# Spectral filter plus dense layers on one core: spectral groups of six PSUM banks, second-layer sums in halves of one bank, a new fixed order

## The chip, the cores and the metric

The kernel runs on one core of a Trainium2 chip. The metric is the device time of one execution in microseconds (us); the time given for a kernel is the median of its timed runs. The times in a profile are those of one further execution, recorded by the hardware profiler.

## The reference

One sequence of 2048 rows and 640 columns goes through a layer norm. The result `xn` feeds two branches, and the sum of both and of `x` is the output (bf16). Branch A is a filter in the frequency domain: a real 2-D Fourier transform over rows and columns, a product with complex weights (2048 x 321), and the inverse transform. Branch B is two dense layers with a gelu between them.

```python
def _A_ref(x, w_r, w_i):
    X = jnp.fft.rfft2(x.astype(jnp.float32), axes=(-2, -1))
    X = X * (w_r + 1j * w_i)
    return jnp.fft.irfft2(X, s=(S, D), axes=(-2, -1)).astype(jnp.bfloat16)
def _B_ref(x, w1, b1, w2, b2):
    h = _gelu(jnp.einsum("bsd,df->bsf", x, w1) + b1)      # 640 -> 1536
    return jnp.einsum("bsf,fd->bsd", h, w2) + b2          # 1536 -> 640
xn = _layernorm(x)
return x + _A_ref(xn, ...) + _B_ref(xn, ...)
```

## The kernel before

All matrix work is done by TensorE (PE) in bf16 with sums in PSUM, which has eight banks of 512 fp32 columns. The 2048 rows are 16 row tiles of 128.

**Head.** SyncE (SP) issues nearly all loads: x in pieces, the first layer's weights `W1` in five pieces of 128 input columns (`load_w1(0)` to `load_w1(4)`), tables, filter weights `Wf`, second-layer weights `W2`. VectorE (DVE) takes the statistics and normalises; row tiles 0 to 3 are transposed by PE (line 710), tiles 4 to 15 by DMA. PE starts with 38 idle matmuls on `warm`.

**First layer** (`ps<-xnT,W` in the profile). Per block of two or four row tiles and per 128 of the 1536 hidden columns, five matmuls of 256 or 512 columns into one bank (`hps`), then a gelu on ScalarE (ACT, line 770). In block 0 the sums advance piece by piece of `W1`.

**Filter.** A length-128 transform (`aps`, with `gtab`) for pairs of row tiles; then, in fixed chain, three kinds of groups, each written by PE to several banks and evacuated to SBUF by VectorE and ScalarE (lines 557 and 558):
- `bps`, the forward width transform (`five` with `etab`): chunks of the sequence (16 in all) against a table of 640 columns. The 640 inputs are four matmuls of 128 rows and 160 columns per chunk, and a remainder of 32 rows, whose matmuls run as 32-row tiles of the array, four at a time.
- `cps`, the forward small transform (`mtab`): matmuls of 32 x 32 and 322 columns on the 16 tiles of the array; VectorE then multiplies by the filter (lines 837, 841).
- `dps`, the inverse small transform (`ntab`), 320 columns; results are transposed by DMA (line 862).

After all of these, `eps` is the inverse width transform (`five` with `getab`), again 16 chunks; VectorE folds its output (lines 887, 892).

`bps` and `eps` work in six groups of two or three chunks (`GROUPS`), `cps` and `dps` in eight groups of 32 matmuls each; every group takes four banks, always among banks 0 to 3. `hps` and the second layer take banks 4 to 7 (`ZONE`).

**Second layer** (`ps<-W,gT`). Per row tile 12 contraction steps of 640 columns, which a bank does not hold, so each step is a matmul of 512 and one of 128 in two banks (`sums`). For nine row tiles (`KEEP`) the sum is formed early (`kps`) and added by VectorE to x + b2 (line 939). At the end a last transform with `htab` goes into the bank (`fps`), VectorE adds (line 948), and SP stores. Row tile 15 is done in pieces of 320, 160 and 160 columns.

**Order.** The program records every operation; `ORDER` gives, by number, the order on each of the five engines, and `Pool.find` gives each operation its banks. Semaphore waits follow from the data and bank dependencies. Each engine works strictly in its order, so that an operation that waits holds up all behind it. Operations of PE among themselves need no wait.

Of the kernel before, what the change touches and what calls it, by code (L numbers as in the profile page):

```python
# [123 lines left out]
class Pool:  # L124
# [34 lines left out]
    "sp": """8 13 14 17 15 16 19 18 21 22 20 27 30 23 26 28 153 155 166 168 32 31 35 46 48 37 179 181 192 194 38 39  # L159
41 34 44 33 29 52 49 40 205 219 221 207 43 42 50 45 51 47 36 54 508 506 505 507 529 531 530 532 554 553 53 555  # L160
556 578 577 580 579 597 642 606 623 633 669 659 678 741 695 750 732 715 766 705 775 782 789""",
    "pe": """7 117 55 119 278 260 122 233 251 242 124 269 234 270 243 252 261 281 254 236 235 279 253 263 272 245 264 273 237 282 275 138
# [8 lines left out]
713 776 777 764 770 778 771 779 772 773 780 783 784 785 786 787""",  # L171
    "act": """12 9 118 56 123 139 258 142 276 259 277 267 250 268 249 292 319 240 241 295 135 313 134 136 322 316 310 307 151 298 301 289
# [3 lines left out]
767 670 609 645 644 680 681 717 753""",  # L176
    "dve": """0 58 57 59 61 62 63 115 116 121 120 66 65 125 67 70 69 137 71 127 126 140 128 130 131 129 144 143 74 76 73 77
# [6 lines left out]
781 788""",  # L184
    "pool": """10 11 3 1 2 60 5 64 6 68 72 79 86 93 4 100 107 25 114 24 589 687 615 625 651 707 661 697 724 743 635 599
759 734 768 671""",
# [29 lines left out]
class Sched:  # L216
# [195 lines left out]
    def emit(self, es, last):  # L412
# [53 lines left out]
def bass_parallel_sum__spectral_gfnet__dense_activation_gelu__prompt_kernel(  # L466
# [21 lines left out]
    with ExitStack() as es:  # L488
# [33 lines left out]
        xb3 = sb("Xb", [128, 6 * 2 * KP])  # L522
# [3 lines left out]
        U2 = sb("U2", [128, 2 * D])  # L526
# [3 lines left out]
        YO, Y2, YF = 0, 6 * D, 9 * D  # L530
# [6 lines left out]
        p_xn, p_x1, p_xf, p_xb, p_y, p_t, p_z, p_u = Pool(2), Pool(1), Pool(2), Pool(2), Pool(2), Pool(2), Pool(2), Pool(3)  # L537
# [453 lines left out]
```

## Time and profile before

| | |
|---|---|
| median of three timed runs | 148.43 us (148.29 to 148.77) |
| span of the profiled execution, first to last instruction | 146.2 us |
| PE / VectorE / ScalarE / GpSimd busy | 140.4 / 110.9 / 81.1 / 23.7 us |
| granted TensorE clock | 1.000 |

The profiled execution's own time is given as its span alone; the timed median is 2.2 us longer. A line of the profile's groups has the line of the code, engine, operation, output<-inputs, shape (partitions x elements), count, then busy us, mean ns of one, and the idle time before it with what ended it. A timeline line has start, length, engine, line and the same names; `x32` joins 32 instructions of a kind. Matmuls are pipelined, so that one of 512 columns has a duration of 379 ns although the next starts much earlier; the ends of matmuls are modelled. All PE work of the kernel but the transposes stands under one line, that of the helper.

### The profile page before, as it was taken

To read this page: it belongs to the slowest core of one execution; us is meant where nothing else is said; L and a number is where in the kernel's file an instruction comes from. 1 tells how busy PE (TensorE), PEld (TensorE's weight loads), DVE (VectorE), ACT (ScalarE), POOL (GpSimd) and SP (SyncE) were. 2 spreads that over 40 slices of the span, in tenths; PEclk is the share of its full clock that TensorE was granted. 3 is DMA by queue.
4 is the path that set the end of the run, shared out by engine and by line. 5 is a ranking of instruction groups with operands and counts; after the bars stand their busy time and mean duration, and the time that the engine had idled before them with its cause. 6 is when DMAs were issued, how large, how long until landed. Compare 5 with 4: busy or idle time off the path is not lost.

```text
span 146.2 us, 4076 instructions
## 1 busy us (share of the span) xinstructions
PE 140.4 (96%) x1702; PEld 91.3 (62%) x1720; DVE 110.9 (76%) x233; ACT 81.1 (55%) x145; POOL 23.7 (16%) x40
## 2 busy tenths in 40 slices
PE   7999999999999999999999999999999999999993
PEld 7788998988455464457554645554446766556572
DVE  1799999999953459799877967982203998998982
ACT  3208999999989769763555633225476655201000
POOL 2330401304200009220200040000063700000000
DMA  4999998998999676968446844462569885103234
GB/s 105 328 394 354 319 164 197 203 175 229 241 238 160 162 195 137 242 126 167 89 92 128 56 95 89 46 142 56 91 129 225 178 188 180 45 4 137 90 135 135
DMA packets 30842, 23.63 MB, mean 162 GB/s; under 512 B 20457, under 2 KB 26857, under 8 KB 30697
## 3 DMA queue, kind: packets, MB, share of 16 engines
q1 hardware_dynamic: 28432, 17.81, 52.6%
q0 software_dynamic: 2368, 5.57, 17.6%
q8 instruction: 13, 0.21, 0.6%
q14 instruction: 5, 0.03, 0.1%
q10 hardware_dynamic: 24, 0.00, 0.0%
HBM read 13.54 MB, written 2.62 MB: 111 GB/s over the span
## 4 chain that ended last, share of the span: by engine, by line
PE 92%; DMA 4%; issue 1%; SPq 1%; DVE 0%
PE ps L546 91%; DMA W<-in_B_w_dram 4%; SPq L541 1%; PE ps L710 0%; DVE W L948 0%
## 5 line engine op out<-in xcount | busy, mean ns | idle before, releaser
L546 PE MATMUL ps<-xnT,W 128*128 128x256 bf16 (+2 forms) x384 | 58.8, 300 | 0.2
L546 PE MATMUL ps<-W,gT 128*128 128x512 bf16 (+3 forms) x380 | 55.7, 292 | 1.6 <-issue 1.1
L546 PEld LDWEIGHTS ps<-W,gT 128*128 128x128 bf16 x396 | 30.3, 98 | 23.4 <-issue 1.9
L546 PEld LDWEIGHTS ps<-xnT,W 128*128 128x128 bf16 x384 | 33.3, 98 | 16.4 <-issue 1.7
L770 ACT ACTIVATE gT<-ps,b1col 128x256 bf16<-128x256 f32 (+1 forms) x72 | 35.3, 558 | 6.8 <-PE ps L546 6.5
L666 DVE BATCH_NORM_STATS2 stats<-X 128x6 f32<-128x320 bf16 x32 | 13.9, 475 | 2.9 <-DMA X<-in_A_x_dram 2.9
L557 ACT ACTIVATE Wf<-ps 128x960 bf16<-128x960 f32 (+1 forms) x8 | 7.0, 902 | 13.7 <-PE ps L546 13.7
L933 POOL DMA_DIRECT2D X<-in_A_x_dram x8 | 7.1, 1132 | 40.5 <-DMA Wf<-in_A_w_r_dram 17.2
L837 DVE TENSOR_TENSOR T<-Y,Wf 128x1288 bf16<-128x1288 bf16 x16 | 12.7, 825 | 0.1
L670 POOL TENSOR_TENSOR rstd<-mv,mhalf 128x2 f32<-128x2 f32 (+1 forms) x10 | 7.2, 717 | 27.5 <-DVE mv L668 27.3
L557 ACT ACTIVATE Xb<-ps 128x960 bf16<-128x960 f32 (+1 forms) x7 | 7.7, 1106 | 6.7 <-PE ps L546 6.7
L933 POOL DMA_DIRECT2D xnT<-in_A_x_dram x8 | 7.5, 1154 | 24.2 <-ACT xnT L915 24.2
L558 DVE CAST Y<-ps 128x644 bf16<-128x644 f32 x8 | 6.5, 827 | 5.4 <-PE ps L546 5.4
L557 ACT ACTIVATE XV<-ps 128x1280 bf16<-128x1280 f32 (+3 forms) x10 | 9.5, 963 | 0.7 <-PE ps L546 0.7
L558 DVE CAST Wf<-ps 128x640 bf16<-128x640 f32 (+1 forms) x4 | 4.0, 990 | 7.6 <-PE ps L546 7.6
L558 DVE CAST Xb<-ps 128x960 bf16<-128x960 f32 (+1 forms) x5 | 5.9, 1178 | 4.1 <-PE ps L546 4.0
L726 DVE TENSOR_TENSOR T<-T 128x512 bf16<-128x512 bf16 (+1 forms) x32 | 8.5, 311 | 0.0
L691 DVE TENSOR_SCALAR T<-X,mv,rstd 128x640 bf16<-128x640 bf16 (+2 forms) x17 | 7.1, 430 | 0.9 <-POOL rstd L670 0.7
L546 PE MATMUL ps<-getab,XV 32*128 32x160 bf16 (+1 forms) x128 | 7.5, 241 | 0.0
L948 DVE TENSOR_TENSOR W<-ps,X 128x640 bf16<-128x640 f32 x8 | 6.5, 822 | 1.1 <-PE ps L546 1.1
L546 PEld LDWEIGHTS ps<-getab,XV 32*128 32x128 bf16 (+1 forms) x128 | 6.5, 146 | 1.3
L887 DVE TENSOR_TENSOR Wf<-Wf 128x960 bf16<-128x960 bf16 (+1 forms) x12 | 7.0, 597 | 0.4 <-ACT Wf L557 0.3
(52 smaller groups left out, 133.4 us busy)
## 6 DMA issues: line engine op xcount, KB each, us to landing
X<-in_A_x_dram POOLq DMA_DIRECT2D x8, 320.0 KB, 4.3
xnT<-in_A_x_dram POOLq DMA_DIRECT2D x8, 320.0 KB, 5.2
out_dram<-W SPq DMA_DIRECT2D x15, 160.0 KB, 1.8
X<-in_A_x_dram SPq DMA_DIRECT2D x7, 320.0 KB, 7.0
W<-in_B_w_dram SPq DMA_DIRECT2D x5, 384.0 KB, 5.9
W<-in_B_w_dram SPq DMA_DIRECT2D x4, 480.0 KB, 7.8
Wf<-in_A_w_i_dram SPq DMA_DIRECT2D x6, 160.5 KB, 5.4
Wf<-in_A_w_r_dram SPq DMA_DIRECT2D x6, 160.5 KB, 4.8
```

What stands on the lines that cost most here:

```text
L546: ins = e.matmul(o_, lhsT=lw, rhs=rh, start=st, stop=sp_, skip_group_check=True)
L557: return e.activation(dst(), src(), ACT.Copy, scale=scale)
L558: return e.tensor_copy(dst(), src())
L666: st_op[c] = K.op([("dve", 0.393)], pr, lambda e, _, c=c, h=h: e.bn_stats(stats[:, c, 6 * h:6 * h + 6], view(X, c * D + H2 * h, [[1, H2]]) ...
L670: K.op([("pool", 0.65)], 500, lambda e, _, a=a, b=b: e.tensor_tensor(out=rstd[:, a:b], in0=mv[:, a:b, 1], in1=mhalf[:, a:b], op=ALU.pow), ...
L691: o = K.op([("dve", 0.066 + (d1 - d0) / 1980.0)], pr, lambda e, _, c=c, n=n, xnv=xnv, d0=d0, d1=d1: e.tensor_scalar(out=xnv(n, d0, [[1, d1 ...
L726: ring_ops.append(K.op([("dve", dve_us(4 * w, 2))], pr, lambda e, _, op=op, x1v=x1v, xfv=xfv, o_=o_, o0=o0, o1=o1, w=w: e.tensor_tensor(ou ...
L770: K.op([("act", act_us(128 * nt, 1))], pr + PRIO["gelu"] + GP[bi], lambda e, _, c0=c0, nt=nt, fc=fc, hps=hps, at=at: e.activation(gT[:, fc ...
L837: filt_ops.append(K.op([("dve", dve_us(4 * KP, 2))], pr, lambda e, _, k=k, Y=Y, TB=TB, pair=pair: e.tensor_tensor(out=view(TT, TB.slot * 8 ...
L887: K.op([("dve", dve_us(320 * n, 2))], pr + 2, lambda e, _, k=k, op=op, yo=yo, y2=y2, n=n: e.tensor_tensor(out=view(Wf, Y2 + y2.slot * 3 * ...
L933: xo_ops[c] = K.op([("pool", 0.9)], 51 - c / 20, lambda e, _, c=c, xov=xov: e.dma_start(xov(0, D), xv[:, c, :], accum_op=ALU.add), reads=[ ...
L948: K.op([("dve", dve_us(w))], 95, lambda e, _, os_=os_, fps=fps, o0=o0, w=w, xov=xov, base=base: e.tensor_tensor(out=view(W1, OST + os_.slo ...
```

## The change

- `GROUPS` becomes four groups of four chunks, each with six banks: chunks 0 to 2 as before in banks 0 to 3 of the group, chunk 3 in two more. It has three evacuations instead of two.
- `cps` and `dps` become four groups of 80 matmuls each, in six banks. The two halves r (or v) of a group, separate groups before, are in one: for half 0 of the pair one of them is split into two parts of half the width (161 or 160 columns), which lie beside the other half's columns in the same banks.
- In such groups, matmuls of two different row tiles of the array come to write the same bank. A matmul raises a semaphore (`DONE`), and PE itself waits for it (`WAIT`) further down its own list.
- The second layer's sums, kept and last, are formed as two halves of 320 columns, each in one bank, with an addition on VectorE for each; the store is still one per row tile.
- `ZONE`: groups take banks 0 to 5; the layers take banks 6 and 7 first, then 4 and 5.
- One filter product buffer instead of two (`p_t`), and other places in SBUF for `U`, `YF`, `Y2`.
- `ORDER` and `CHAIN` are new. Among much else, SP loads x's rows 2 and 3 ahead of the first piece of `W1`, and ScalarE's `preload_act_table` (operation 9) stands near the end of its list instead of at the start; the built program has three table loads on ScalarE where it had one: before the first evacuation, before the first gelu, and this one.

```diff
 ORDER = {
-    "sp": """8 13 14 17 15 16 19 18 21 22 20 27 30 23 26 28 153 155 166 168 32 31 35 ...
+    "sp": """8 13 17 14 15 19 18 16 21 22 23 31 27 20 30 28 38 155 153 166 168 48 179 ...
-    "act": """12 9 118 56 123 139 258 142 276 259 277 ...
+    "act": """12 118 123 56 139 142 285 307 286 292 ... 564 460 ... 801 566 831 9 466 572 574 ...
...
-GROUPS = [(0, 2), (2, 3), (5, 3), (8, 3), (11, 3), (14, 2)]
+GROUPS = [(0, 4), (4, 4), (8, 4), (12, 4)]
-ZONE = {"hps": [(4, 8)], "bps": [(0, 4)], "cps": [(0, 4)], "dps": [(0, 4)],
-        "eps": [(0, 4)], "fin": [(4, 8), (0, 4)], "fps": [(4, 8)], "tps": ANY, "aps": ANY}
+ZONE = {"hps": [(6, 8), (4, 6)], "bps": [(0, 6)], "cps": [(0, 6)], "dps": [(0, 6)],
+        "eps": [(0, 6)], "kps": [(6, 8), (4, 6)], "fin": [(4, 8), (0, 4)], "fps": [(6, 8), (4, 6)], ...}
-CHAIN = "b1 b0 c01 c00 b2 c10 d01 c11 d00 b4 b3 d10 d11 c20 c21 b5 c30 d20 d21 c31 d30 d31".split()
+CHAIN = "b0 c0 b1 c1 d0 b2 d1 c2 b3 c3 d2 d3".split()
...
+                    if o_ == "done":
+                        ins.then_inc(inner, 1)
+                        seen[0] += 1
+                    elif o_ == "wait":
+                        e.wait_ge(inner, seen[0])
...
+        def five(slot, lhs, tab):
+            def to(g, i):
+                return psb(slot + (g if i < 3 else 4 + g // 2), [[1, Q4]], Q4 * (i if i < 3 else g % 2))
+            def rem(g, i):
+                return [(to(g, i), lhs(i, 4, 32 * g, 32), tab[32 * g:32 * g + 32, 4 * Q4:5 * Q4], False, True)]
+            out = [(to(g, i), lhs(i, g, 0, 128), ...) for g in range(4) for i in range(4)]
+            out += rem(0, 3) + rem(2, 3) + DONE + rem(1, 0) + rem(3, 0)
+            for k in range(2):
+                out += rem(0, k) + rem(1, k + 1) + rem(2, k) + rem(3, k + 1)
+            return out + rem(0, 2) + rem(2, 2) + WAIT + rem(1, 3) + rem(3, 3)
...
+            def c_list(P=P, cps=cps):
+                def go(r, pps, bank, off, k0, w, first):
+                    return [(psb(cps.slot + bank(pp, hi), [[1, w]], off, 64 * qq + 32 * (lo ^ pp), 32), ...)
+                            for v in range(2) for pp, qq, hi, lo in tiles if pp in pps]
+                K2 = KP // 2
+                return (go(1, (0,), lambda pp, hi: 2 + hi, KP, K2, K2, True) + DONE + go(0, (0, 1), lambda pp, hi: 4 * pp + hi, 0, 0, KP, True)
+                        + go(1, (0,), lambda pp, hi: hi, KP, 0, K2, False) + WAIT + go(1, (1,), lambda pp, hi: 2 + hi, 0, 0, KP, False))
...
-                    second(c, kps, 0, D, pr, ...)
+                    for o0 in (0, H2):
+                        kps = Buf(f"kps{c}_{o0}", psum, 1, ZONE["kps"])
+                        second(c, kps, o0, H2, pr, ...)
...
-                for o0, w in [(0, D)] if c < 15 else [(0, H2), (H2, Q4), (H2 + Q4, Q4)]:
+                for o0, w in [(0, H2), (H2, H2)] if c < 15 else [(0, H2), (H2, Q4), (H2 + Q4, Q4)]:
```

`dps` has a list of the same build as `c_list`, with widths 160 and 320.

More of the change, by code (lines that the diff above doesn't have):

```diff
@@ new lines, in bass_parallel_sum__spectral_gfnet__dense_activation_gelu__prompt_kernel @@
+            zone[f"c{P}"] = pe([("small", 0.66)], PRIO["pc"] - P / 2, c_list, reads=in_xb + [B_xbpad, B_m], writes=[cps])
+            c_ev = []
+            for r, pp in ((0, 0), (0, 1), (1, 1), (1, 0)):
+                Y = Ys[pp]
+                if r and not pp:
+                    dst = lambda Y=Y: view(Yb, Y.slot * 4 * KP + KP, [[2 * KP, 2], [KP // 2, 2], [1, KP // 2]])
+                    src = lambda cps=cps: psb(cps.slot, [[512, 2], [1024, 2], [1, KP // 2]], KP)
+                else:
+                    dst = lambda Y=Y, r=r: view(Yb, Y.slot * 4 * KP + r * KP, [[2 * KP, 2], [1, KP]])
+                    src = lambda cps=cps, pp=pp, r=r: psb(cps.slot + (2 if r else 4 * pp), [[512, 2], [1, KP]])
+                c_ev.append(K.op([("act", act_us(644)), ("dve", dve_us(644))], PRIO["pc"] - two[pp] / 5, copy(dst, src),
+                                 reads=[cps], writes=[Y], after=[c_ev[0], c_ev[2]] if r and not pp else ()))
@@ new lines, in bass_parallel_sum__spectral_gfnet__dense_activation_gelu__prompt_kernel, with d_list, go @@
+            dps = Buf(f"dps{P}", psum, 6, ZONE["dps"])
+            def d_list(P=P, Zs=Zs, dps=dps):
+                def go(v, pps, bank, off, g0, ng, first):
+                    return [(psb(dps.slot + bank(pp, qq), [[1, Q4 * ng]], off, 64 * hi + 32 * lo, 32),
+                             part(ntab, 64 * qq + 32 * (lo ^ pp), 32, (P == pp == qq == hi == lo == 0) * 96 + 32 * ((0, 2), (1, 0))[v][r], [[1, 32]]),
+                             part(Zb, 64 * qq + 32 * (lo ^ pp), 32, Zs[pp].slot * 4 * KP + (2 * hi + r) * KP + v + g0, [[1, ng], [2, Q4]]), first and r == 0, r == 1)
+                            for r in range(2) for pp, qq, hi, lo in tiles if pp in pps]
+                return (go(0, (0,), lambda pp, qq: 2 + qq, H2, 1, 1, True) + DONE + go(1, (0, 1), lambda pp, qq: 4 * pp + qq, 0, 0, 2, True)
+                        + go(0, (0,), lambda pp, qq: qq, H2, 0, 1, False) + WAIT + go(0, (1,), lambda pp, qq: 2 + qq, 0, 0, 2, False))
@@ new lines, in bass_parallel_sum__spectral_gfnet__dense_activation_gelu__prompt_kernel, with evac @@
+            d_ops.append(pe([("small", 0.69)], PRIO["ipc"] - P / 2, d_list, reads=Zs + [B_n], writes=[dps]))
+            zone[f"d{P}"] = d_ops[-1]
+            d_ev = []
+            for v, pp in ((1, 0), (1, 1), (0, 1), (0, 0)):
+                U = Us[pp]
+                def evac(e, name, U=U, v=v, uv=uv, dps=dps, pp=pp):
+                    for o_, w in ((0, 128), (512, 32)):
+                        if v or pp:
+                            src = lambda: psb(dps.slot + (4 * pp if v else 2), [[512, 2], [Q4, 2], [1, w]], o_ // 4)
+                        else:
+                            src = lambda: psb(dps.slot, [[512, 2], [1024, 2], [1, w]], H2 + o_ // 4)
+                        ins = copy(lambda: uv(U, o_ + 2 * w * v, [[D, 2], [w, 2], [1, w]]), src)(e, name)
+                    return ins
+                d_ev.append(K.op([("act", act_us(512) + act_us(128)), ("dve", dve_us(512) + dve_us(128))], PRIO["ipc"] - two[pp] / 5, evac,
+                                 reads=[dps], writes=[U, B_us[pp]], after=a_ops + ring_ops + ([d_ev[0], d_ev[2]] if not v and not pp else [])))
```

163 lines of the change are left out of this document (72 added, 91 removed), and 38 rows, old and new, of the table ORDER.

## The prediction

> **What bounds the kernel now.** I read the page first: engines, slices, chain.
>
> ```profile
> PE 140.4 (96%) x1702; PEld 91.3 (62%) x1720; DVE 110.9 (76%) x233; ACT 81.1 (55%) x145; POOL 23.7 (16%) x40
> ...
> PE 92%; DMA 4%; issue 1%; SPq 1%; DVE 0%
> PE ps L546 91%; DMA W<-in_B_w_dram 4%; SPq L541 1%; PE ps L710 0%; DVE W L948 0%
> ```
>
> TensorE is busy 96% of the span and is 92% of the chain that ended last. Then the waits of PE alone:
>
> ```profile
> PE ps L546 <- issue: 1.3, 8, 0.2
> ```
>
> After the first microseconds PE waits for no other engine: what is left is 1.3 us of "issue". So from about 8 us to the end the time is PE's stream itself, and a change is worth what it takes out of that stream or pushes into it. The chain in order of time shows the head, which is not PE's:
>
> ```profile
> 2.68 5.39 DMA W<-in_B_w_dram
> ...
> 8.12 2.35 PE ps L546 x28
> ```
>
> PE stands until the second of the five pieces of the first layer's weights has landed, at 8.07.
>
> **Halves of one bank: 0.** Per contraction step a second-layer row tile was 512 + 128 columns and is 320 + 320. PE's columns and matmul count stay (180 + 180 become 360). By shape:
>
> ```profile
> L546 PE MATMUL ps<-W,gT 128*128 128x512 bf16 x164 | 48.6, 379 | 0.0
> L546 PE MATMUL ps<-W,gT 128*128 128x128 bf16 x180 | 39.4, 219 | 1.6 <-issue 1.1
> L546 PE MATMUL ps<-W,gT 128*128 128x320 bf16 x12 | 2.3, 299 | 0.0
> L558 DVE CAST Xb<-ps 128x960 bf16<-128x960 f32 x4 | 5.0, 1252 | 2.5 <-PE ps L546 2.4
> L558 DVE CAST Xb<-ps 128x640 bf16<-128x640 f32 x1 | 0.9, 881 | 1.6 <-PE ps L546 1.6
> ```
>
> 379 + 219 = 598 and 2 x 299 = 598 ns: nothing. VectorE adds each half by itself: 24 more instructions (9 kept sums, 15 last sums).
>
> ```profile
> 130.92 1.55 DVE L948 TENSOR_TENSOR W<-ps,X 128x640 bf16<-128x640 f32 x2
> ```
>
> Two adds of 640 take 1.55, one 0.82 (the page's mean), so the next starts 0.73 after the last. The page's 0.49 for 320 less the same overlap of 0.09 gives two halves 0.81: 0.08 more per tile, 2 us of VectorE in all, beside PE. I price it at 0 and keep 1 us for the tail, where VectorE is already fullest.
>
> **Width transforms, 6 + 6 groups become 4 + 4: -0.9.** Whole groups, each from its first matmul to PE's next one:
>
> ```profile
> 65.87 1.31 PE L546 MATMUL ps<-etab,XV 128*128 128x160 bf16 x24
> 67.12 0.39 PE L546 MATMUL ps<-W,gT 128*128 128x512 bf16 x1
> 79.76 0.97 PE L546 MATMUL ps<-etab,XV 128*128 128x160 bf16 x16
> 80.66 0.28 PE L546 MATMUL ps<-xnT,W 128*128 128x256 bf16 x1
> 113.37 1.37 PE L546 MATMUL ps<-getab,XV 128*128 128x160 bf16 x24
> 114.67 0.39 PE L546 MATMUL ps<-W,gT 128*128 128x512 bf16 x1
> ```
>
> Three chunks 1.25, two chunks 0.90: 0.35 per chunk and 0.20 per group (etab); with 1.30 for three, getab has 0.25 per group. The chunks stay 16 per table, so two groups fewer save 2 x 0.20 + 2 x 0.25 = 0.90.
>
> **The wait inside each of these groups: +0.55.** The two remainder matmuls behind WAIT may start only when the second remainder matmul of the group is finished; queued behind them is all of PE's stream. No row shows PE waiting for itself, so I bound it by its parts:
>
> ```profile
> 5.63 0.22 PE L710 MATMUL ps<-ident,T 128*128 128x128 bf16 x1
> 5.88 0.39 ACT L557 ACTIVATE xnT<-ps 128x256 bf16<-128x256 bf16 x1 [3.15 <-PE ps L710]
> 6.32 0.40 PE L546 MATMUL ps<-xnT,W 128*128 128x128 bf16 x4
> ...
> L546 PE MATMUL ps<-etab,XV 32*128 32x160 bf16 x64 | 2.2, 231 | 0.0
> ```
>
> PE's end to ACT's start: 0.03. ACT's end (6.27) to PE's start: 0.05. So the matmul waited for (0.23) plus 0.08 gives 0.31 after the remainder began; without the wait, the last round starts after three rounds of 0.07 (0.35 less four main matmuls of 0.069, which are a row of twelve below), at 0.21. Between 0 (if the modelled end is late) and 0.10; I take 0.07, since ACT did start 0.03 behind a modelled end. Eight groups: 0 to 0.8, taken 0.55. The Trainium skill (Advanced Engine Details and Errata, section Network/Comms) puts a sequencer's reading of a semaphore at 50 to 100 ns; the trace's 0.05 agrees with its lower end, and by its upper end these waits would be 0.4 dearer, an estimate from that page.
>
> **Small transforms, 8 + 8 groups become 4 + 4: +0.4.** This looks like the larger saving and I think it is none. One group of 32 with the first layer around it, in three windows:
>
> ```profile
> 99.83 0.38 PE L546 MATMUL ps<-xnT,W 128*128 128x512 bf16 x1
> 100.14 0.37 PE L546 MATMUL ps<-Z,ntab 32*32 32x320 bf16 x16
> 100.14 0.46 PE L546 MATMUL ps<-Z,ntab 32*32 32x320 bf16 x17
> 100.14 0.52 PE L546 MATMUL ps<-Z,ntab 32*32 32x320 bf16 x32
> 100.59 0.39 PE L546 MATMUL ps<-W,gT 128*128 128x512 bf16 x1
> 103.74 5.14 PE L546 MATMUL ps<-xnT,W 128*128 128x512 bf16 x23
> 108.72 0.38 PE L546 MATMUL ps<-W,gT 128*128 128x512 bf16 x1
> 142.64 0.99 PE L546 MATMUL ps<-W,gT 128*128 128x160 bf16 x12
> 143.47 0.23 PE L546 MATMUL ps<-Wf,htab 128*128 128x160 bf16 x1
> ```
>
> A 512 takes 4.98 / 23 = 0.216, so PE was free at 100.05 and the group cost 0.54: 0.09 to switch, a wave of 16 tiles, the second wave starting between 100.29 and 100.30 (0.156 after the first), and 0.29 from there to PE's next. By 0.83 / 12 = 0.069 for 160 columns, 320 stream in 0.133, so a tile is used again about 0.02 late.
>
> Two such groups: 1.08 (the first kind some 0.02 less each). The new group has the same multiplications in eight waves, but the parts for pair half 0 in rows of half width use only 8 of 16 tiles. In order, starts at 0, 0.09 (half width, same tiles), 0.18, 0.335 (full), 0.49, 0.58 (half), then the last part on the other 8 tiles, 0.61 and 0.765, then 0.27 to the next: 1.03, with the switch 1.12 to 1.13. So one switch of some 0.2 goes and some 0.25 of half-empty waves comes: +0.05 a group, 8 groups +0.4. Its own inner wait, for the part that began at 0.09, ends at about 0.12 + 0.23 + 0.08 = 0.43, before 0.61: nothing. If tiles are reused with no gap, starts are 0, 0.07, 0.13, 0.27, 0.40, 0.47, 0.49, 0.63, and the group costs 0.98: -0.65 for all eight. Range -0.65 to +0.55.
>
> **The head: +0.4.** SyncE's queue now has the third load of X ahead of the first weight piece.
>
> ```profile
> 1.73 0.43 SPq L541 DMA_DIRECT2D W<-in_B_w_dram  x1
> 2.21 0.43 SPq L541 DMA_DIRECT2D X<-in_A_x_dram  x1
> ...
> DMA to landing us min/median/max: 4.4/4.4/4.4
> ...
> DMA to landing us min/median/max: 5.0/5.0/5.0
> ...
> 6.67 0.50 PE L546 MATMUL ps<-xnT,W 128*128 128x128 bf16 x6
> ...
> 7.18 0.87 PE L546 MATMUL ps<-xnT,W 128*128 128x128 bf16 x12
> ```
>
> The piece landed at 1.73 + 4.4 = 6.1, that X at 7.2. Swapped, the piece lands at about 7.2 and the second piece still at 8.07. Before, PE did 4 + 6 + 12 = 22 first-layer matmuls by then; the new order has 12 in front of its first wait for the second piece: 10 x 0.054 (a quarter of a 512) = 0.54 behind. Some 0.24 is made up: the 28 matmuls after 8.12 are 18 of 128 and 10 of 256, 18 x 0.054 + 10 x 0.108 = 2.05, and took 2.35 in the chain's row (0.16 of it the last one's pipeline), since PE stood for the later pieces, twice; the new stream has left-over work there. That leaves 0.3. ScalarE's explicit table load is moved from the front to its last tenth, and the built program loads a table ahead of the first gelu instead:
>
> ```profile
> 1.45 1.28 ACT L595 ACT_TABLE_LOAD   x1 [1.45 <-PEq L976]
> ...
> 12.88 4.50 ACT L770 ACTIVATE gT<-ps,b1col 128x256 bf16<-128x256 f32 x12
> ```
>
> It cost 1.28 before PE had anything for ScalarE; now it sits behind the fourth evacuated transpose (about 11.9). Gelus then run from 13.2, one per 0.37, each 0.49 long (4.50 = 11 x 0.365 + 0.49). Counting PE's new order from 8.13 at these prices, it needs the banks of the second and third at 14.3 and 14.6 (ready 14.1 and 14.5) and of the sixth at 15.5 (ready 15.6): +0.1. The explicit load, near 104, has ten second-layer steps of 3 x 0.135, 4.0, in front of its gelu's user, and takes 1.28 of that: 0.
>
> **Six banks: +0.3.** While a group holds six, layers have two. Between the first width group and its small transform PE has 10 matmuls of 256 and 5 of 512, 10 x 0.108 + 5 x 0.216 = 2.16; the evacuation in series on VectorE (640, then 960) is 0.88 + 1.25 - 0.09 and handoffs of 0.08, 2.12. If that cover of 0.04 is gone, PE stands in front of the small transform. Several of the 12 spectral groups up to the last small one are that close; I take 0.3, from 0 to 2.4 (0.2 at each). The single product buffer of the filter is written and read by VectorE in order anyway: 0.
>
> **Sum.** -0.90 + 0.55 + 0.40 + 0.40 + 0.30 = +0.75. The profiled execution spans 146.2; the timed median is 148.43, 2.2 more, which I carry over: 148.4 + 0.8 = 149.2.
>
> **The rivals.**
> *Switches win (not slower):* tile reuse costs no gap and inner waits are hidden: -0.90 - 0.65 + 0.40, 147.3. It decides from a small group under about 1.02 at WAIT costs under 0.03. For it: ends of matmuls are modelled. Against: the 0.156 between waves.
> *Gelu starved:* the change of table holds ScalarE for twice the row's 1.28. If gelus begin over 0.2 later than 13.2, PE stands for a bank from 14.3 on, and ScalarE, which has no gap then (twelve in 4.50), gives nothing back; 1.3 later makes 149.2 + 1.3 = 150.5. Nothing in the profile speaks for it: the one load had its 1.28 and no work close behind. The Trainium skill (ScalarE: Activation LUTs, What ACT_TABLE_LOAD costs) adds a drain of about 1.38 to a load of 1.28 at each switch to another set; the row agrees on the load, and no run here shows the drain.
> *Two banks are too few:* each of 12 groups stops PE 0.2, or VectorE's 2 us of extra adds show in the tail: 149.2 + 2.1 = 151.3. For it: covers of 0.04. Against: before, 5 matmuls of 512, 1.08, cover one evacuation of 0.88 and 0.08 of handoffs, 0.12 to spare, and PE never waited.
> *It does not do what it says:* no; the built order has 8 groups of small and 8 of width matmuls.
>
> **Numbers.** Forecast 0.47 (its own range 148.5 to 149.9), switches win 0.20, gelu starved 0.11, two banks 0.17, more of everything 0.05. A measurement here tells 0.3%, 0.45 us, from no change. Faster: the 0.20 and 0.03 of the forecast's lower edge, 0.23; same (148.0 to 148.9): 0.20 of the forecast; slower 0.57. The range 147.4 to 151.2 leaves out about 0.1 on either side.
>
> **What would show it.** A small group from free PE to next PE at 1.1 and not 0.95; the last pair of remainder matmuls in a width group 0.07 to 0.10 behind the round; first-layer matmuls from 7.2; gelus from 13.2; PE's waits still without ACT and DVE. PE waiting over 2 us for those two, or small groups under 1.0, proves me wrong.

## The result, and the profile after

| | time, us | against before |
|---|---|---|
| before, median of four runs | 148.6 | |
| changed kernel, median of four runs | 153.5 (153.43 to 154.22) | 1.0337 [1.0293, 1.0381] |
| forecast | 149.2 (147.4 to 151.2) | |

The change makes the kernel 4.9 us slower. The direction of the forecast is right; its size, +0.8 us, is far too small. A ratio, here and below, leaves out executions more than 1.5% above the fastest of their kernel, so that it can differ from the quotient of the medians. The profiled execution spans 151.3 us where the one of before spanned 146.2. The page of the changed kernel, engines and chain:

```profile
PE 144.2 (95%) x1848; PEld 104.0 (69%) x1848; DVE 114.4 (76%) x250; ACT 82.8 (55%) x146; POOL 23.2 (15%) x40
...
PE 83%; DMA 9%; DVE 3%; ACT 2%; issue 1%; SPq 1%; POOL 0%; DVEq 0%
PE ps L558 82%; DMA X<-in_A_x_dram 6%; DMA xnT<-T 3%; DVE stats L679 1%; ACT gT L783 1%; PE ps L723 1%; DVE T L704 1%; SPq L711 1%; DVE mv L681 0%; ACT Y L570 0%; POOL X L969 0%; DVE X L976 0%; DVE W L986 0%; DVEq L433 0%
```

TensorE was 92% of the chain that ended last and is 83%. Two transfers have come into the chain that were not in it: the addition of x (6%) and the transposes of row tiles (3%). TensorE's waits, which after the first microseconds had held only "issue":

```profile
PE ps L558 <- DVE warm L575: 1.1, 1, 1.1
PE ps L558 <- DVE X L976: 1.1, 1, 1.1
PE ps L558 <- ACT gT L783: 0.8, 2, 0.6
PE ps L558 <- DMA xnT<-T: 0.7, 1, 0.7
PE ps L723 <- DVE T L704: 0.6, 2, 0.4
PE ps L558 <- issue: 0.2, 1, 0.2
```

The first line is the start of the program, as before. The next three are new, 2.6 us. The wait for row tile 1 (line 723) was 0.3 and is 0.6. The chain in order of time (start, length) shows where two of them come from, and the timeline the instructions around the second:

```profile
18.28 4.98 DMA xnT<-T
23.25 0.09 issue
23.35 2.14 PE ps L558 x18
...
58.52 6.41 DMA X<-in_A_x_dram
...
65.03 0.50 DVE X L976
...
65.58 47.41 PE ps L558 x723
```

```profile
57.90 6.32 POOL L969 DMA_DIRECT2D X<-in_A_x_dram  x7 [20.06 <-ACT Y L570]
65.03 0.49 DVE L976 TENSOR_TENSOR X<-ps,X 128x320 f32<-128x320 f32 x1 [1.80 <-DMA X<-in_A_x_dram]
```

Row tiles 4 and 5 arrive transposed at 23.25 us (21.66 before), row tile 7 at 27.33 (24.36 before), and TensorE stands 0.90 and 0.81 us there, counted from start to start of its matmuls (0.74 and 0.64 in the waits, which count from a modelled end). The two waits booked under ScalarE's gelu, 0.64 and 0.20, each end about 0.1 us behind a transpose that has landed, of row tile 7 and of row tile 11 (33.18). Later VectorE waits 1.80 us for x of row tile 3. Its transfer may start only when the last filter weights have landed, and they land at 57.60. Before, they land at 54.48 (the 54.67 that an expectation below names is the table `ntab`), and the same transfers start 3.1 us earlier:

```profile
54.78 3.63 POOL L933 DMA_DIRECT2D X<-in_A_x_dram  x4 [17.18 <-DMA Wf<-in_A_w_r_dram]
```

VectorE's addition frees a bank, and TensorE stands 1.1 us for that bank. From 69 us on no stand of that size is left.

The parts that the prediction priced, in the rows that answer to its own. Second-layer halves by shape, width groups (etab, getab) with the matmul behind them, a small group, the head:

```profile
L558 PE MATMUL ps<-W,gT 128*128 128x320 bf16 x372 | 57.1, 299 | 1.1 <-DVE X L976 1.1
```

```profile
72.48 1.75 PE L558 MATMUL ps<-etab,XV 128*128 128x160 bf16 x32
74.17 0.72 PE L558 MATMUL ps<-W,gT 128*128 128x320 bf16 x4
113.08 1.88 PE L558 MATMUL ps<-getab,XV 128*128 128x160 bf16 x32
114.89 0.58 PE L558 MATMUL ps<-W,gT 128*128 128x320 bf16 x3
93.74 1.11 PE L558 MATMUL ps<-Xb,mtab 32*32 32x161 bf16 x80
94.79 0.61 PE L558 MATMUL ps<-xnT,W 128*128 128x256 bf16 x4
```

```profile
6.76 0.51 PE L558 MATMUL ps<-xnT,W 128*128 128x128 bf16 x6
11.92 1.28 ACT L783 ACT_TABLE_LOAD   x1
13.21 6.83 ACT L783 ACTIVATE gT<-ps,b1col 128x256 bf16<-128x256 f32 x18
```

A width group of four chunks takes 1.69 (etab) and 1.81 (getab; the other three 1.78). A small group takes 1.05 from its first matmul to TensorE's next, 1.14 with the 0.09 ahead of it; those with `ntab` take 1.18 by the same measure.

### The profile page after: what moved, and what is told of

Read it like the earlier page. It is cut to its first block, busy times and chain, and to the rows that moved or that the text cites. A ratio compares the mean times of both kernels' runs of the same rounds, so it can differ in the third digit from the quotient of the medians.

```text
span 151.3 us, 4367 instructions
## 1 busy us (share of the span) xinstructions
PE 144.2 (95%) x1848; PEld 104.0 (69%) x1848; DVE 114.4 (76%) x250; ACT 82.8 (55%) x146; POOL 23.2 (15%) x40
## 4 chain that ended last, share of the span: by engine, by line
PE 83%; DMA 9%; DVE 3%; ACT 2%; issue 1%; SPq 1%; POOL 0%; DVEq 0%
PE ps L558 82%; DMA X<-in_A_x_dram 6%; DMA xnT<-T 3%; DVE stats L679 1%; ACT gT L783 1%; PE ps L723 1%; DVE T L704 1%; SPq L711 1%; DVE mv L681 0%; ACT Y L570 0%; POOL X L969 0%; DVE X L976 0%; DVE W L986 0%; DVEq L433 0%
## 5 line engine op out<-in xcount | busy, mean ns | idle before, releaser
L558 PE MATMUL ps<-W,gT 128*128 128x320 bf16 (+1 forms) x396 | 59.1, 295 | 1.1 <-DVE X L976 1.1
L558 PEld LDWEIGHTS ps<-W,gT 128*128 128x128 bf16 x396 | 37.2, 98 | 18.3 <-DVE X L976 1.6
L976 DVE TENSOR_TENSOR X<-ps,X 128x320 f32<-128x320 f32 x16 | 7.7, 489 | 9.0 <-PE ps L558 7.2
L570 ACT ACTIVATE Y<-ps 128x644 bf16<-128x644 f32 x10 | 7.0, 706 | 6.7 <-PE ps L558 4.7
L571 DVE CAST Xb<-ps 128x640 bf16<-128x640 f32 (+1 forms) x6 | 6.3, 1060 | 3.8 <-PE ps L558 3.8
L986 DVE TENSOR_TENSOR W<-ps,X 128x320 bf16<-128x320 f32 x16 | 7.3, 485 | 1.7 <-PE ps L558 1.7
L986 DVE TENSOR_TENSOR W<-ps,xnT 128x320 bf16<-128x320 f32 (+1 forms) x17 | 7.4, 466 | 1.5 <-PE ps L558 1.3
L571 DVE CAST XV<-ps 128x1280 bf16<-128x1280 f32 (+3 forms) x5 | 5.2, 1061 | 3.6 <-PE ps L558 3.6
L558 PE MATMUL ps<-T,htab 128*128 128x320 bf16 (+1 forms) x33 | 8.0, 295 | 0.0
L558 PE MATMUL ps<-getab,XV 128*128 128x160 bf16 (+1 forms) x128 | 7.4, 241 | 0.1
```

The lines of the kernel that those rows point to most:

```text
L558: ins = e.matmul(o_, lhsT=lw, rhs=rh, start=st, stop=sp_, skip_group_check=True)
L570: return e.activation(dst(), src(), ACT.Copy, scale=scale)
L571: return e.tensor_copy(dst(), src())
L976: kept_ops.append(K.op([("dve", dve_us(H2))], 30, lambda e, _, kps=kps, xov=xov, o0=o0: e.tensor_tensor(out=xov(o0, H2), in0=psb(kps.slot, ...
L986: K.op([("dve", dve_us(w))], 95, lambda e, _, os_=os_, fps=fps, o0=o0, w=w, xov=xov: e.tensor_tensor(out=view(W1, OST + os_.slot * D + o0, ...
```

## The experiments

All times are medians, set against runs of the kernel before on the same chip. "Less by the ratios" is counted from the changed kernel's 1.0337. That same kernel measured again (changed_again, below) has 1.0214 by the ratio, 1.8 us less, though its medians agree (153.5 and 153.88): so what a single edit gains against it is uncertain by as much. Where an order is edited, banks and buffers are held to those of the changed kernel, in all runs but filter_loads_later. Numbers are those of `ORDER`, of which only the stretches that change are shown.

**First four: one suspect each.**

filter_loads_later:

```diff
 "sp"   -28 38 155 153 166 168 48 179 181 192 194 33
        +28 155 153 166 168 48 179 181 192 194 38 33
 "pool" -79 25 86 93 100 6 107 24
        +79 86 93 100 6 107 25 24
```

> Two loads of filter weights (operation 38 on SyncE, 25 on GpSimd) are moved from ahead of the transposes of row tiles 4 to 7 to behind those of row tiles 8 to 11 (38) and behind the statistics of row tile 12 (25). In the changed kernel these transposes land at 23.25 and 27.33 us where they landed at 21.66 and 24.36 before, and TensorE stands 0.90 and 0.81 us in front of them. My theory, that the two loads hold the transposes up, expects both gaps gone or below 0.3 each, and 1.2 to 2.0 us less than the changed kernel. Rival 1, VectorE's later normalisation or SyncE's own waits set the landing: under 0.4 us less. Rival 2, the gain is given back further on because the loads of filter weights then end later than 57.60 and the first additions of x with them: gaps gone, but under 1.0 us less in total.

152.32 us, 1.0257 [1.0224, 1.0289]: 1.2 us less by the ratios. Both gaps in front of the transposes are gone (row tile 7 lands at 25.79), but VectorE's addition of x now holds TensorE for 1.4 us. This does not show that the two loads hold the transposes up: in the profile of changed_again, where nothing is edited, row tile 7 lands at 25.22, there is no gap either, and the addition holds TensorE for as long. Theory and rivals stay undecided by this run.

x_added_early:

```diff
-            xo_ops[c].deps += WL + list(TD.values())
+            xo_ops[c].deps += ([] if c in (0, 3) else WL) + list(TD.values())
```

> The transfers that add x for row tiles 0 and 3 no longer wait for the last load of filter weights (that wait is no data dependency). In the changed kernel they are issued at 57.90 and 58.52, and the second lands just ahead of VectorE's addition at 65.03, for whose bank TensorE has stood 1.1 us. My theory, that this transfer is what TensorE waits for, expects the wait of TensorE for the addition gone and 0.9 to 1.3 us less. Rival 1, the bank is late for another reason (VectorE has its evacuations first): under 0.3 less. Rival 2, the two transfers, issued near 45 us among the loads of filter weights, push those and the product behind them back: no gain, or a loss of up to 1 us.

152.25 us, 1.0252 [1.0224, 1.0279]: 1.3 us less by the ratios. The wait for the addition is gone. In its place TensorE waits for the last piece of the second layer's weights, which lands at 56.54 instead of 55.22:

```profile
PE ps L558 <- DMA W<-in_B_w_dram: 1.0, 1, 1.0
```

This wait is as long as the one that it replaces (1.02 against 1.05 us), so the gain does not come from there. The profiled execution also has no stand in front of the transposes, which the edit does not touch. That the time fell by as much as theory named looks like luck.

small_interleaved, in words (`d_list` likewise; v is the contraction half; A and A2 are the two parts of half width, B the half of the pair that stays whole, C the full-width rest behind the wait):

```diff
-half-width A (v 0, 1), DONE, B on 16 tiles (v 0, 1), half-width A2 (v 0, 1), WAIT, C (v 0, 1)
+A v0, B v0 pair half 1, A v1, DONE, B v0 pair half 0, B v1 pair half 1, B v1 pair half 0, WAIT, C v0, A2 v0, C v1, A2 v1
```

> Inside each of the eight small transforms the same 80 matmuls stand in another order: a wave of half width on eight tiles is always next to a wave of full width on the other eight. A group takes 1.13 to 1.14 us now, two groups of before took 1.04 to 1.08. My theory, half-empty waves cost 0.09 to 0.17 a group, expects a group at 0.97 to 1.04 and 0.8 to 1.3 us less in all. Rival, a group is bound by the rate at which its 80 instructions start (8.3 ns each in its middle, 0.66 in all) or by the wait inside it, which comes no earlier in this order: a group stays over 1.09 and the time within 0.4 us.

153.48 us, 1.0307 [1.0263, 1.0351]. The groups do what the theory says: six of the eight take 0.92 to 0.94 plus 0.09 where there were 1.05 to 1.09 plus 0.09. The time can't show it here: the executions scatter from 152.45 to 155.42, by more than the 1.0 us in question. The same edit is tried again below, in a kernel without the stalls.

table_first:

```diff
 "act"  -12 118 123 ... 566 831 9 466
        +12 9 118 123 ... 566 831 466
```

> ScalarE's explicit table load goes back to the front of its list (banks and buffers are held at those of the changed kernel). The gelus then need not wait for a load of 1.28 us at 11.92. My prediction priced this part at 0.1 us: 0 to 0.2 us less. Rival, ScalarE is the one that holds TensorE in 20 to 34 us (the waits of 0.8 us stand under ScalarE's gelu): 0.8 us less or more.

153.56 us (151.61 to 154.06), 1.0316 [1.0270, 1.0362]: no difference that can be told. Its profile, of the execution at 151.61, showed something else. In the chain by time, table_first and, for comparison, the later changed_again:

```profile
8.40 3.20 PE ps L561 x28
```

```profile
8.04 1.67 PE ps L558 x28
```

The same 28 matmuls take 3.20 instead of 1.67 us: those of 128 columns start 107 ns apart instead of 56, called the half rate below. The windows row from 8 to 11 us of table_first has the granted clock at 0.53 (before the DMA share), that of all_mended below at 1.00:

```profile
8.00:11.00 3.00, 3.00 (x32) 3.00 (x31) 3.00 (x12) 0.17 (x1) 1.10 (x2) 0.53 1.02 400
```

```profile
8.00:11.00 3.00, 3.00 (x48) 2.85 (x46) 2.97 (x11) 0.75 (x2) 1.10 (x2) 1.00 1.03 405
```

That execution is the fastest of its six all the same, and it has none of the later stands.

**Next four: the order, and one part alone.**

loads_in_old_turn (with `25` on GpSimd as above):

```diff
 "sp"   -28 38 155 153 166 168 48 179 ... 194 33 49 46 ... 47 29 26 35 50 45 43 32 40 42 51
        +28 26 155 153 166 168 32 179 ... 194 33 48 38 49 46 ... 47 29 35 50 45 43 40 42 51
```

> Changed kernel with its loads back in the turn that they had before, as far as that goes: two of the four pieces of the second layer's weights (operations 26 and 32) are issued ahead of and right behind the transposes of row tiles 4 to 7, and filter weights (38, 48, and 25 on GpSimd) behind. My theory is that both stalls, 0.90 + 0.81 us in front of late transposes and 1.1 us in front of the addition of x, have one cause, the turn of the loads on SyncE: in the runs so far the last filter weights land at 56.4 to 59.5 us (54.67 before), and x is added only behind them. It expects the last filter weights to land by 56, no wait of TensorE for the additions, and 1.5 to 2.8 us less than the changed kernel (ratio to before 1.015 to 1.024). Rival 1, the larger weights ahead of the transposes hold these up as much as the filter weights did, or more: gaps of 0.8 us and over remain there and the ratio stays above 1.025. Rival 2, the wait for x's addition is set by seven such transfers queued at once, not by when they start: that wait stays at 1 us.

151.56 us (149.81 to 151.93), 1.0176 [1.0113, 1.0238]: 2.4 us less by the ratios. The last filter weights land at 55.0 and TensorE waits for no addition, as theory says. No gap in front of transposes is left either, but the profiled execution has the half rate in its head, so that TensorE comes there later; of the transposes it shows nothing.

head_in_old_turn:

```diff
 "sp"   -8 13 17 14 15     "dve"  -115 116 66 121 65 70 67 69 120 71
        +8 13 14 17 15            +115 116 121 120 66 65 70 67 69 71
```

> Changed kernel with the first piece of the first layer's weights again ahead of the third load of x on SyncE, and VectorE normalising row tile 1 and copying row tile 0's transpose ahead of the statistics of row tile 2. In the runs so far TensorE stands 0.6 to 2.1 us at 5 to 9 us for row tile 1, because VectorE, working in order, waits with it for x's third load (5.64 to 6.57). My theory expects that wait under 0.3 us, the first-layer matmuls from 6.4 to 6.8 instead of 6.8 to 8, and 0.5 to 1.0 us less. Rival, everything that TensorE gains in the head it loses at 22 to 34 us, where it then stands longer for the transposes of row tiles 4 to 11 (the gaps there grow by as much): under 0.2 us less.

152.20 us, 1.0174 [1.0103, 1.0245]. TensorE's stand for row tile 1 is 0.3 us, where it is 0.4 in the first profile of the changed kernel and 0.7 to 1.2 in the others with its head; but there are 0.3 us for transposes behind it, 1.4 for the addition of x and 0.9 for another addition near 113 us. Theory named 0.5 to 1.0 us less; it is 1.3 by the medians, and 2.4 by the ratios, which rest on three executions here. The waits behind the head are as the rival says. What the head is worth this run can't tell.

all_mended is loads_in_old_turn, head_in_old_turn, small_interleaved and table_first in one.

> Changed kernel with four edits together: loads in their old turn, head in its old turn, small transforms interleaved, table load at the front. If the stalls are what the 5 us consist of (head 0.5 to 1, transposes 1.7, addition of x 1.1, half-empty waves 1.0, table 0.1), their sum of 4.4 to 4.9 us goes and the kernel comes to the time of before, ratio 0.998 to 1.005. Rival 1, the changed kernel still pays for waits inside its width transforms and longer small ones and for its order: ratio 1.008 to 1.015. Rival 2, the loads bound the first 60 us, and what TensorE gains ahead of that it stands for later: ratio above 1.015.

149.35 us (148.81 to 150.52), 1.0066 [1.0037, 1.0096]: 4.0 us less than the changed kernel by the ratios, and not back to before. It lies between theory (up to 1.005) and rival 1 (from 1.008), nearer to theory; rival 2 falls. Its rows for the addition of x and a small group:

```profile
53.19 6.33 POOL L973 DMA_DIRECT2D X<-in_A_x_dram  x7 [17.10 <-ACT gT L775]
```

```profile
60.61 0.49 DVE L980 TENSOR_TENSOR X<-ps,X 128x320 f32<-128x320 f32 x1
```

```profile
89.60 0.98 PE L550 MATMUL ps<-Xb,mtab 32*32 32x161 bf16 x80
90.52 0.72 PE L550 MATMUL ps<-xnT,W 128*128 128x256 bf16 x5
```

The seven transfers of x start 4.7 us earlier, the addition stands at 60.61 without a wait, and the group takes 0.92.

halves_alone (kernel of before, its order and banks):

```diff
-                    return [(o0, 512 - o0), (512, o0 + w - 512)] if w > 512 else [(o0, w)]
+                    return [(o0, H2), (o0 + H2, H2)] if w > 512 else [(o0, w)]
```

(with the two halves in two banks and an addition on VectorE for each)

> Kernel of before, its order and banks untouched, with one part of the change alone: each second-layer step is 320 + 320 columns in two banks instead of 512 + 128, and VectorE adds each half by itself. The prediction priced this at 0, with up to 1 us in the tail: ratio 0.998 to 1.004, a pair of halves at 2 x 0.136 us of TensorE's stream as 512 + 128 were at 0.216 + 0.054. Rival, VectorE's further additions (2 us in all) hold banks longer and TensorE with them: 1.005 to 1.014.

148.36 us, 0.9989 [0.9958, 1.0021]. This part of the change costs nothing that can be told.

**Then: the parts taken out of the mended kernel.**

changed_again is the changed kernel with no edit.

> The changed kernel as it is, on the chip of the next three, to have them against it and not only against the kernel before, and to have a second profile of its head. Expected 1.030 to 1.036 of before. In three of seven profiles of kernels with its head, TensorE's matmuls of 128 columns started 107 ns apart instead of 56 from about 8 to about 11 us, behind a stand of 0.9 to 1.2 us for row tile 1; whether this one has it is open. Where it has it, I expect the stand in front of the transposes at 23 and 27 us gone, since TensorE comes there later; where it has not, I expect that stand, 0.9 and 0.8.

153.88 us (150.79 to 155.06), 1.0214 [1.0122, 1.0305]. This kernel has no single time: the ratio rests on its two lowest executions, and by the medians it is 1.037, so that one lies below the expected 1.030 to 1.036 and the other above. The profiled one (span 150.9) has neither the half rate nor a stand at 23 or 27 us, so my condition for the stand was wrong. Against the first profile it is 1.8 us earlier at the first width group and has lost 1.3 of that by 115 us:

```profile
64.21 0.49 DVE L976 TENSOR_TENSOR X<-ps,X 128x320 f32<-128x320 f32 x1 [1.93 <-DMA X<-in_A_x_dram]
```

The addition of x comes at 64.21, again behind its transfer, and TensorE waits 1.4 us for it.

mended_no_inner_wait:

```diff
+                at = 2 if i == 3 and g % 2 else i
-                return [(to(g, i), lhs(i, 4, 32 * g, 32), ...)]
+                return [(to(g, at), lhs(i, 4, 32 * g, 32), ...)]
-            out += rem(0, 3) + rem(2, 3) + DONE + rem(1, 0) + rem(3, 0)
+            out += rem(0, 3) + rem(2, 3) + rem(1, 0) + rem(3, 0)
-            return out + rem(0, 2) + rem(2, 2) + WAIT + rem(1, 3) + rem(3, 3)
+            return out + rem(0, 2) + rem(2, 2) + rem(1, 3) + rem(3, 3)
```

(DONE and WAIT are left out of the width transforms, and two remainder matmuls of each group add to chunk 2's columns instead of chunk 3's, so that its sums there are wrong.)

> all_mended without the wait inside the width transforms: of the two remainder matmuls behind it, each adds to columns of a bank that its own row tile writes anyway, so that no two row tiles share a bank (this part of the output is a wrong sum; count and shape of the matmuls stay). Theory: the wait costs TensorE what the groups show, 0.09 in each of four groups with etab and 0.14 in each of four with getab, 0.9 us in all: a remainder at 0.39 and 0.43 instead of 0.48 and 0.57, and 0.7 to 1.0 us less than all_mended, at or below before (ratio 0.997 to 1.002). Rival 1, my prediction's term: 0.55 less. Rival 2, VectorE's evacuations or loads take it back: under 0.3 less.

148.34 us, 0.9995 [0.9967, 1.0022]: 1.0 us less than all_mended, and level with before. Its width groups:

```profile
68.43 1.66 PE L550 MATMUL ps<-etab,XV 128*128 128x160 bf16 x32
70.02 0.85 PE L550 MATMUL ps<-W,gT 128*128 128x320 bf16 x5
```

```profile
108.50 1.74 PE L550 MATMUL ps<-getab,XV 128*128 128x160 bf16 x32 [0.46 <-DMA XV<-gtab]
110.17 0.45 PE L550 MATMUL ps<-W,gT 128*128 128x320 bf16 x2
```

1.59 and 1.67 instead of 1.69 and 1.81. The theory holds, rival 1 and rival 2 fall.

mended_small_as_changed is all_mended without the edit of small_interleaved.

> all_mended but with the small transforms in the changed kernel's own order. Theory: eight groups of 1.14 instead of 1.01 us, 0.13 each: 0.8 to 1.1 us more than all_mended (ratio 1.011 to 1.016). Rival, what small transforms gain is stood for later anyway: within 0.3 of all_mended.

150.25 us, 1.0107 [1.0063, 1.0150]: 0.9 us more by the medians, 0.6 by the ratios, whose intervals overlap. In the profiles its eight groups take 0.91 us more than those of all_mended, and TensorE's last matmul ends 0.86 us later. The half-empty waves are on the path.

mended_table_late is all_mended without the edit of table_first.

> all_mended but with the explicit table load where the change put it, so that a table is loaded in front of the first gelu (1.28 us, at about 11.9). Prediction: gelus from about 13.2 and 0.1 us more. Rival, starved gelus: with the head in order TensorE reaches the gelus' banks earlier than in the changed kernel and stands for them, 0.4 us or more, seen as waits of TensorE for ScalarE's gelus at 13 to 20 us.

149.68 us, 1.0073 [1.0043, 1.0102], against 1.0066: 0.1 by the ratios, 0.3 by the medians, less than can be told. The gelus run from 13.31, and TensorE has no wait for them at 13 to 20 us. One of 0.2 us at 31.6 is booked under them and ends 0.09 behind the transpose of row tile 11. The gelus are not starved.

mended_head_as_changed and mended_loads_as_changed are all_mended without the edits of head_in_old_turn and with the change's turn of the loads.

> all_mended but with the head's order as the change has it (x's third load ahead of the first weights; VectorE takes its statistics ahead of row tile 1). Theory: TensorE stands about 1 us for row tile 1 at 6 to 7, and in part of the executions its matmuls then run at half rate to 10.5 or 11.5 us, 1.2 to 1.5 us more: 0.6 to 2.2 us more than all_mended (ratio 1.011 to 1.021), with executions in two heaps. Rival, the loads bound the first 60 us and hide the head: within 0.3 of all_mended.

> all_mended but with the loads in the turn of the change. Theory: transposes of row tiles 4 to 7 land late (a stand of up to 1.7 us) and the additions of x behind the last filter weights make VectorE's second addition, and TensorE behind it, late to about 65.5 us where all_mended had none: 1.5 to 3.0 us more than all_mended (ratio 1.017 to 1.027). Rival, with head, table and small transforms mended this turn costs nothing by itself: within 0.5.

150.82 us (149.51 to 151.12), 1.0148 [1.0103, 1.0194], and 152.02 us (149.82 to 153.53), 1.0141 [1.0070, 1.0213]. By the ratios each costs 1.1 to 1.2 us more than all_mended's 1.0066; by the medians over all their executions 1.5 and 2.7. The first has its executions in two heaps, one at 149.51 and six from 150.47 on. Only the 149.51 has a trace, so that the upper ones have the half rate is not shown; one of the six has a mean granted clock of 0.989, the other five 1.000. The trace has no half rate, and a stand for row tile 1 of 1.0 us that hardly costs time by itself:

```profile
PE ps L723 <- DVE T L704: 1.2, 2, 1.0
```

The traced execution of the second is its fastest, at 149.82. It has none of theory's wait for the addition of x. Its waits, booked under gelus, are 0.5 us each for the transposes of row tile 7, which land at 25.95 (25.56 in all_mended), and of row tile 11 (32.14 against 30.34). Where its slower executions stand is not shown.

mended_head_filled (ten idle matmuls more, as operation 869):

```diff
 "pe"   -7 117 119 122
        +7 117 119 869 122
```

> mended_head_as_changed with ten more idle matmuls of 128 columns in TensorE's order, between the transposes of row tile 0 and those of row tile 1, where it stands for VectorE. Theory: the half rate comes from that stand; filled for 0.55 to 1.1 us, the matmuls behind it start 56 ns apart in all executions, and the time lies in one heap, 0.3 to 1.0 us above all_mended (the stand itself stays). Rival, the half rate has another cause: two heaps as in mended_head_as_changed, and 0.3 us more for the idle matmuls where they hold the transposes up.

149.35 us (148.90 to 150.67), 1.0087 [1.0059, 1.0114]: 0.9 us less than without the ten matmuls by the ratios (1.5 by the medians), though they do no work and row tile 1 is transposed at 7.04 as against 7.14. Nine of twelve executions lie below 150. So the late row tile costs little by itself, and what costs seems to be that TensorE is idle while it waits. The half rate behind such a stand would do that. Neither kernel's trace has it, but the mean granted clock of the other executions points the same way: it is 0.989 in eleven of the 45 executions of kernels with the changed head (in two of these, of table_first and small_interleaved, the trace shows the half rate), and below 0.995 in none of the 74 of the other kernels tried, this one among them, and in one of the kernel before. It does not mark every case: loads_in_old_turn has the half rate in its trace and a mean of 1.000.

**What follows together.** The ladder from below: all parts mended and no inner wait 0.9995; the inner wait back 1.0066; the small transforms as changed 1.0107; the order as changed 1.0337. In us of 148.4: 1.05, 0.6 and 3.4; by the medians 1.0, 0.9 and 3.3 (3.6 with changed_again). The third is spent by 69 us: from the first small inverse group to TensorE's end the changed kernel takes 79.91 us and mended_small_as_changed 79.83. How it divides between head and loads stays open: put back singly they cost 1.2 and 1.1 by the ratios, 1.5 and 2.7 by the medians, and each may cover or bring out part of the other. No version here beats before: with all its sums right the kernel stays 0.7% slower, and without the wait it is even. It is even, and not faster by the 0.86 us that its width groups save, because TensorE still stands. Apart from the start of the program its waits in mended_no_inner_wait are 1.5 us (0.8 in the head, 0.5 for the first getab group's input, 0.2 for a transpose); in halves_alone they are 0.3.

## Why the prediction was right or wrong

**What bounds the kernel.** "From about 8 us to the end the time is PE's stream itself": right for the stream of before and from 69 us on, wrong for the new order until then. With the old turn of the loads the stream had nothing to wait for; the sum took this as given for the new turn too and counted only what is in the stream. This is the step that failed: a wait for loads stood in the sum at nothing, and the order as changed costs 3.4 us. What the sum did price in the stream, +0.05 us for width groups, inner wait and small transforms, comes to about +0.9 in the rows. The 1.3 us of "issue" in the waits of before are most likely records that its trace lacks: it has 164 second-layer matmuls of 512 beside 180 of 128, and the trace of halves_alone, with 18 matmuls more for the same work, has no such wait.

**Halves: 0.** Right. 299 ns each in the rows, 0.9989 in halves_alone, and nothing in the tail.

**Width groups: -0.90.** Right. Adding up the distances between starts of matmuls, the width matmuls of halves_alone take 13.83 us of TensorE and those of mended_no_inner_wait 12.97: 0.86 less.

**The inner wait: +0.55.** Mechanism right, term too small: 0.09 in an etab group and 0.14 in a getab group, 0.9 in all, against a bound of 0.8, and 1.0 on the chip. It eats the whole saving. The price was made from etab's matmul and the shorter handoffs of the trace. The estimate by the upper end of what the Trainium skill states (Advanced Engine Details and Errata, section Network/Comms) was 0.4 more, 0.95; the 0.9 of the groups agrees with it.

**Small transforms: +0.40.** Mechanism right, and shown by undoing it: filling the half-empty waves takes 0.13 to 0.15 from each group. The size was half of what it is. The mtab group came out at 1.14 against 1.12 to 1.13, but its two predecessors are 1.04 and not the 1.08 that I used for both kinds; the ntab group is 1.18. So each is 0.10 dearer than the two that it replaces, 0.8 in all, above the end of my range at 0.55. That end allowed for no dearer group than the one I had drawn.

**The head: +0.4.** The step that failed here is that only SyncE's first loads and ScalarE's table were followed. First-layer matmuls start at 6.76 (forecast 7.2) and gelus at 13.21 (forecast 13.2), and the table costs 0.1 by the ratios, as forecast and less than can be told. But VectorE's new order takes the statistics of row tile 2 ahead of row tile 1's normalisation, so TensorE's transposes of row tile 1 wait for x's third load: 0.4 us in this profile, 0.7 to 1.2 in others, and in some of them the half rate behind it. Put back into all_mended, the head's order costs 1.2 us by the ratios, 1.5 by the medians.

**Six banks: +0.3.** Not there: in all_mended, with the same banks, TensorE waits for no bank. A wait of 0.2 us that is booked under a gelu ends 0.09 behind the transpose of row tile 7 (25.56). The bank that TensorE stands for at 65 us in the changed kernel is late because of a transfer, not of an evacuation. The rival "two banks are too few" gave 151.3, the nearest to the result, by a mechanism that isn't there.

**What was not in the sum at all.** The turn of loads behind the head. SyncE's and GpSimd's new lists put filter weights ahead of the transposes, and three of the four pieces of the second layer's weights into the last batch. I had the lists and stopped at the third entry. The last filter weights then land at 55.5 to 59.5 us in the eight profiled kernels with the change's turn (two loads apart in one of them), and at 52.9 to 55.1 in the seven with the old one; behind them come x, an addition, a bank and TensorE. TensorE stands 1.1 to 1.7 us for that addition in five of the eight, and 0.6 in one of the seven. The transposes of row tiles 4 to 7 are not late as a rule: row tile 7 lands at 24.3 to 27.3 with the change's turn and at 24.1 to 25.6 with the old one. By its own test ("PE waiting over 2 us for those two") the forecast is wrong: 2.5 us stand under VectorE and ScalarE, 0.8 of it in truth transposes.

**Rivals.** "Switches win" fell with the inner wait and with small groups of 1.14 and 1.18, and "gelu starved" with mended_table_late. The Trainium skill (ScalarE: Activation LUTs, What ACT_TABLE_LOAD costs) adds a drain of about 1.38 us to a load at each switch to another set. Here the load starts at 11.92, 0.02 after the copy ahead of it has ended, and the gelu 0.01 behind the load, so this trace does not show one.

## What to carry to other kernels

Where an order is replaced, the queues of loads are part of the price: for every load that changes its turn, write down what lands behind it and who is first to need that, down to the bank that is not freed. Fewer and larger groups save switches only if nothing inside them waits: the waits in eight groups ate what four switches had saved. And a stall can't be priced by taking it out of a kernel that has several, nor without measuring that kernel twice: out of the changed kernel the loads and the head seemed worth 2.4 us each by the ratios, put back into the mended one 1.1 and 1.2.

## What the runs showed of the hardware that was not expected

Behind a stand of 0.7 to 1.2 us in the head, TensorE ran at half its rate for 3.2 to 3.4 us in some executions and not in others: 107 against 56 ns from start to start of 128 columns, seen in three of the eight profiles with the changed head (table_first, small_interleaved, loads_in_old_turn). The length of the stand does not decide it: x_added_early stands 1.2 us and has the full rate behind. In loads_in_old_turn the granted clock of these microseconds still reads 1.00, so the distance of the starts tells it and the clock's row need not. The Trainium skill (TensorE: Matmul & The Clock Gate, Part 1) has the two rates and says that the full one is granted after about 3.4 us of work and lost after an idle stretch of that length, by a window that runs free of the kernel. The rates agree. So does the length: in table_first the rate changes at 4.8, 8.2 and 11.6 us, 3.4 apart. The stand seen here is much shorter than that, behind idle matmuls that ran at the half rate throughout (loads_in_old_turn) or at first (the other two).

Small matmuls of 32 x 32 tiles can be mixed in width at little loss, if a wave of half width on eight tiles always stands next to one of full width on the other eight: 80 matmuls then take 0.92 to 0.94 us to TensorE's next, where the same 80 in separate waves take 1.05 to 1.09.
